# W1's transposes moved into another stage, K's stores on other queues, a third row buffer for W2 in a fused training step (long convolution gated with a squared-ReLU MLP)

## The chip, the cores and the metric

The kernel runs on one core of one Trainium2 chip. The metric is the device time of one execution in microseconds (us). TensorE is PE, its weight loads are PEld, VectorE is DVE, ScalarE is ACT, GpSimd is POOL and SyncE is SP. SP does no arithmetic here: it issues DMAs, as POOL and ACT also do beside their own work. Each engine takes its instructions in the order of its own queue, so an instruction that waits holds up all that stand behind it.

## The reference, cut to what matters

The input is a sequence of L = 2048 rows with D = 448 channels. A gate mixes the output of a long convolution (a state space model with 256 states per channel, whose kernel K is summed from powers and applied by FFT) with that of a dense block of hidden width F = 1792. Forward and all gradients are computed.

```python
g = sigmoid((u * gate_w).sum(-1, keepdims=True))
dt = exp(log_dt); P = exp((dt * A)[:, :, None] * arange(L))
K = einsum("dn,dnl,dn->dl", C, P, dt * B).real
a = irfft(rfft(pad(u)) * rfft(pad(K)))[:L] + u * Dskip
r = relu(x @ w1 + b1)
b = (r * r) @ w2 + b2
out = g * a + (1 - g) * b
_out, _vjp = jax.vjp(f, u, A_re, A_im, B_re, B_im, C_re, C_im, log_dt, Dskip, w1, b1, w2, b2, gate_w)
return out, *_vjp(grad_out)
```

Inputs and outputs are bf16.

## The kernel before

**Two jobs in one order.** The convolution and the dense block do not depend on each other until the end, so their work is interleaved by hand. The dense block is a Python generator `dense()` of small steps: `first_layer` (hidden rows r, written to DRAM as `rT_d`), `second_layer` (gradients of the hidden rows, written as `dhT_d`, and of the weights), `project(0, w2n)` (the output of the block) and `project(1, w1T)` (its gradient with respect to x). Each step has an entry in the list `cost`. `D_(want)` runs steps until their summed cost reaches a wanted share; the last `TAILN` = 6 steps are kept back and run by `N_(TAILN)` late in the tail. One projected tile is two steps of 7 matmuls each.

**The loop over chunks.** The 448 channels are worked off in 14 chunks c of 32. A period is a list of tokens, `PERIOD`, one for each chunk:

```python
PERIOD = """YS SA Z0 D R Y0 Y1 D Z1 Y2 D R Y3 Z2 D NX Y4 D Z3 KM KO
            LY WD P0 D P1 D X0 FY0 S FY1 FY2 X1 D R X2 D""".split()
```

YS and Y0 to Y4 build the table Y for chunk c on DVE (L1059, L1018 to L1021); there is one tile Y. KM makes K's terms from it with 128 matmuls (L1082), KO evicts them on ACT (L1089). LY issues four transposing DMAs of Y on SP (L1106) into the tile R; the next chunk's YS waits until they have landed. Z0 to Z3 multiply the transposed tables of the chunk before (matmuls L1144, eviction on ACT L1150); P0 and P1 are their products on DVE (L1159, L1161), S sums them (L1176, L1181). X and FY build the next tables. D stands for the dense steps.

**Queues and held loads.** The loads that the dense steps need are issued by `defer(key, f)`: it puts them into a list that `release()` empties at the tokens R and LY, so that the loads come out on SP's queue behind LY's transposes or ahead of them. Row loads for `project` are `load_rows2` (L881), with keys of 98 and more. `project` squares the loaded rows on ACT (L893) for its first half, evicts a tile on ACT (L908) and multiplies with w2 (natural) or with w1T, the transposed W1. Before, w1T is made by seven transposing DMAs on SP (`load_w1t`, L925), one each 256 columns of W1, spread over the tiles 0 to 5 of the first projection; the first is issued at the end of `second_layer`. The second layer turns W2 by transposes on PE from row buffers that POOL loads (`load_w2`, `turn_w2`); there are two such buffers. The squares of the first rows (L858) are done at the end of `second_layer`.

**The stores of K.** `k_store` writes K to DRAM (`k_d`, L1098) in two parts: after chunk 9 on POOL, and after the last chunk on POOL and SP, two each. `reload_k` reads it back in another layout (L1368, L1374, on both queues), `again` copies rows on DVE that are needed twice (L1440), one addition puts Dskip in (L1509), and `fwd1` transforms the result (L236, stores to gd). The last chunk's `T` token turns Y on PE instead of by DMA, and its Z (`back_z` with banks, L1148) is evicted by ACT and DVE in turn.

**The tail.** After fwd1 stand the `TAILN` dense steps, the loads of gd (`load_s1`, L250), the last P0 and P1, the parameter gradients `param_grads` (called in steps by `Pg`, L1459 to L1493) and `fwd2` (matmuls L260, evictions L211 and L222), whose results are multiplied (L1547, L1548) and transformed back.

Of the kernel before, what the change touches and what calls it, by code (L numbers as in the profile page):

```python
# [19 lines left out]
P = 128  # L20
# [3 lines left out]
DT = 4  # L24
# [295 lines left out]
def kernel(ctx, tc, A_u, A_A_re, A_A_im, A_B_re, A_B_im, A_C_re, A_C_im, A_log_dt, A_Dskip,  # L320
# [22 lines left out]
    dhT_d = dscr("dhT_d", F * L)  # L343

# [276 lines left out]
    w2b = [SB[:, 10240:10688], SB[:, 8208:8656]]  # L621
    w2T = [SB[:, 9216 + 512 * i:9728 + 512 * i].rearrange("p (a f) -> p a f", a=DT) for i in range(2)]
# [16 lines left out]
    def release():  # L639
        while held:  # L640
            held.pop(0)[1]()
# [79 lines left out]
    def first_layer():  # L721
# [6 lines left out]
        for j in range(FT):  # L728
# [29 lines left out]
    def load_w2(j):  # L758
        G_.dma_start(w2b[j % 2], bass.AP(tensor=B_w2.tensor, offset=B_w2.offset + j * P * D, ap=[[D, P], [1, D]]))

    def turn_w2(j):
        ps = K.ps(BK["t"], [P, DT, P], bf16)
        for dt in range(DT):
            for h in range(1 if dt < 3 else 2):
                T_.transpose(ps[64 * h:64 * h + DSZ[dt], dt], w2b[j % 2][:, dt * P:dt * P + DSZ[dt]], ident[:], tile_position=(0, 64 * h))
        S.copy(w2T[j % 2], ps[:])
        if j + 2 < FT:
            load_w2(j + 2)
# [51 lines left out]
    def second_layer():  # L820
# [44 lines left out]
        defer(99, lambda: load_w1t(0))  # L865
# [18 lines left out]

    def project(w, ws):
# [3 lines left out]
        def square(n, x):  # L889
            if w == 0:  # L890
                for b in slot_of(n):
                    v = b[:, :, P * x:P * x + P]
                    S.activation(v, v, ACT.Square)  # L893
        for x in range(2 * w):
            square(0, x)
        for n in range(8):
            for x in range(2):
# [11 lines left out]
                if n < 7:  # L909
                    square(n + 1, x)  # L910
# [4 lines left out]
                if x == 1:  # L915
# [4 lines left out]
                    if i < HP - 1:  # L920
                        defer(100 + i, lambda m=i + 1: load_w1t(m))
                yield

    def load_w1t(jp):
        nc.sync.dma_start_transpose(out=w1T[:, 2 * jp:2 * jp + 2], in_=B_w1[:, 256 * jp:256 * jp + 256])  # L925
# [13 lines left out]
    TAILN = 6  # L939
# [153 lines left out]
    def k_store(c):  # L1093

        if c in (9, NCH - 1):
            c0, n = (0, 5) if c == 9 else (5, 2)
            for g in range(NG):
                (G_ if c == 9 or g % 2 == 0 else nc.sync).dma_start(bass.AP(tensor=k_d, offset=112 * g + 16 * c0, ap=[[48 * D, NA], [D, NY], [1, 16 * n]]),  # L1098
# [34 lines left out]
    def back_z(c, yt, j, banks=None):  # L1133
# [12 lines left out]
        if banks:  # L1146
            for t in range(2):
                (S.copy if t == 0 else V.tensor_copy)(run(zbs[c, h][:, 0:1], 16 * (j % 2) + 1024 * t, [64, NA], [32, 2], [1, 16]), run(psz[t][:, 0:1], 0, [1, NA], [NA, 2], [32, 16]))  # L1148
# [143 lines left out]
    PERIOD = """YS SA Z0 D R Y0 Y1 D Z1 Y2 D R Y3 Z2 D NX Y4 D Z3 KM KO LY WD P0 D P1 D X0 FY0 S FY1 FY2 X1 D R X2 D""".split()  # L1292
    nd = PERIOD.count("D")

    def token(o, c):
# [13 lines left out]
        elif o == "R":  # L1309
            release()  # L1310
        elif o[0] == "L" and new:
# [41 lines left out]
    period(1, "YS Y0 Y1 Y2 Y3 Y4 D D D SP D WP KM KO D Z0 D Z1 D P0 Z2 D".split(), -nd)  # L1353
# [55 lines left out]
    G_.dma_start(Pt[:, 4096:7168], cdr["M2"].ap()[:, 0:3072])  # L1409
    Yf = Y[:].rearrange("p w t b -> p (w t b)")  # L1410
    slots = [KW[:, 7168:10752], KW[:, 10752:14336], R2[:, 7168:10752], R2[:, 12288:15872], hv[:, 0:3584], hv[:, 3584:7168], P2[:, 0:3584], Yf[:, 0:3584], Yf[:, 3584:7168]]
# [11 lines left out]
    period(NCH - 1, [o for o in PERIOD[:i] if o != "SA"])  # L1423
    D_(goal)
    release()
    assert done == total - TAILN
# [5 lines left out]
    for j in range(4):  # L1432
        back_z(NCH - 1, YTs[NCH - 1][j], j, NT[2 * (j % 2):2 * (j % 2) + 2])
    K.pairs = 3

    def again(p0, cp, j, m, i, step=1, rep_=1):
# [3 lines left out]
        cp(run(dst[:, 0, 0:1], 0, [step * D, rep_], [D, m], [1, D]), run(src[:, 0, 0:1], 0, [0, rep_], [D if step == 1 else 0, m], [1, D]))  # L1440
    Gt = Pt[:, 0:7168].rearrange("p (t d) -> p t d", d=D)
    tmps = [DBx[:, 7168:8192], hv[:, 7168:8192], Yf[:, 7168:8192], SB[:, 5120:6144], R2[:, 10752:11776], R2[:, 11776:12288]]
# [56 lines left out]
    again(64, V.tensor_copy, 2, 1, 0)  # L1499
    again(64, V.tensor_copy, 4, 1, 0, 4, 3)  # L1500
    again(64, V.tensor_copy, 5, 2, 1, 4, 3)
    again(64, V.tensor_copy, 7, 1, 3, 4, 3)
    for j, m, i in ((8, 4, 0), (4, 2, 0), (6, 1, 1), (12, 2, 2), (14, 1, 1), (15, 1, 7)):
        again(32, V.tensor_copy, j, m, i)
    got = {32: [0, 1, 2, 3, 0, 1, 1, 7, 0, 1, 2, 3, 2, 3, 1, 7], 64: [0, 1, 0, 3, 0, 1, 1, 3] + [0, 1, 1, 3] * 2}
    for p0, w in ((32, {0: 0, 8: 1, 4: 2, 12: 3, 16: 7}), (64, {0: 0, 8: 1, 16: 3})):
        assert [w[int(vp[p0, j]) - LT * p0] for j in JO] == got[p0]
    xv = xs.rearrange("p l (g c e) -> p l c g e", g=NG, e=16)
    V.tensor_tensor(out=xv[0:1, 0], in0=xv[0:1, 0], in1=dsk_bc[0:1].rearrange("o (c g e) -> o c g e", g=NG, e=16), op=ALU.add)  # L1509
# [186 lines left out]
```

## Time and profile before

| | us |
|---|---|
| median of 3 runs | 752.05 |
| fastest and slowest of them | 748.56, 754.67 |
| the profiled execution | 752.95 |
| its span | 751.1 |
| mean granted TensorE clock | 0.904 of full speed |

The span runs from the first to the last instruction of the profiled execution; the rest of its time lies around it. Times in the profile's views are counted from the span's start. Roughly, the loop over chunks runs from 214 to 603, with the second layer in the periods up to c = 7 and the two projections after them; the tail runs from 603 to the end. In the views, a group is given by line, engine, operation, and `out<-in` with the names of the tiles; several tiles share one buffer, so that w1T and the row buffers appear as S, U, P and F, and the transposed Y as R. A name such as `R<-Y` after an arrow is the instruction that ended a wait.

Some groups of the page for orientation (busy time in us and the mean of one in ns, then the idle time of the engine just before them):

```profile
L1018 DVE TENSOR_TENSOR Y<-Y,F 128x1024 bf16<-128x1024 bf16 (+3 forms) x70 | 48.0, 686 | 2.7
L905 PE MATMUL psN<-S,U 128*128 128x448 bf16 x140 | 29.0, 358 | 1.8 <-DMA S<-in_B_w_dram 1.8
L1059 DVE COPY Y<-rec 128x256 bf16<-128x256 bf16 x14 | 10.6, 755 | 21.5 <-DMA R<-Y 15.5
```

### The profile page before, as it was taken

The numbers are of one execution on the slowest core, as the hardware profiler recorded it, in microseconds if no ns is written. First come the engines' busy times: TensorE is split into PE (matmuls) and PEld (weight loads), VectorE is DVE, ScalarE is ACT, GpSimd is POOL, SyncE is SP. The second block draws the span as 40 slices with busy tenths as digits, with TensorE's granted clock in tenths as the row PEclk, the third lists the DMA queues.
The fourth block names the chain that finished last, engine by engine and source line by source line (L and its number), as shares of the span: only waits on it lengthen the run. The fifth ranks groups of instructions, "written<-read, shape, count | busy, mean of one in ns | idle before, by whom it ended". The sixth has DMA issues, their size and how long they took to land.

```text
span 751.1 us, 20458 instructions
## 1 busy us (share of the span) xinstructions
PE 621.1 (83%) x8556; PEld 337.4 (45%) x8597; DVE 564.7 (75%) x932; ACT 512.1 (68%) x873; POOL 171.6 (23%) x296
## 2 busy tenths in 40 slices
PE   5947968779999787999989997888969978687666
PEld 2412323323346453665665664555545664433111
DVE  1495586675698456899898997988699877959473
ACT  2895958587887576778777777777634535597555
POOL 2251112111263220211201201110100332411543
PEclk9887967879999899999999999999989988799758
DMA  9997586827773997997997989999999966998995
GB/s 211 220 280 243 195 294 240 291 103 285 283 263 134 249 256 214 200 249 203 219 209 216 240 137 240 244 198 245 218 186 234 276 165 199 389 333 297 333 327 147
DMA packets 197115, 177.77 MB, mean 237 GB/s; under 512 B 121534, under 2 KB 174039, under 8 KB 196895
## 3 DMA queue, kind: packets, MB, share of 16 engines
q1 hardware_dynamic: 173823, 113.11, 61.9%
q0 software_dynamic: 15632, 44.48, 19.3%
q10 hardware_dynamic: 7568, 18.88, 6.7%
q8 instruction: 67, 1.10, 0.6%
q14 instruction: 25, 0.20, 0.1%
HBM read 83.95 MB, written 64.32 MB: 197 GB/s over the span
## 4 chain that ended last, share of the span: by engine, by line
PE 28%; DMA 12%; DVE 10%; ACT 7%; issue 7%; POOL 1%; SPq 0%; POOLq 0%; ACTq 0%; DVEq 0%
PE psN L905 5%; PE psS L1176 5%; DMA R<-Y 3%; PE psN L661 3%; PE psX L1082 3%; PE psN L697 3%; DVE Y L1021 2%; DVE Y L1018 2%; DVE F L1019 2%; DMA U<-in_A_u_dram 2%; DMA S<-in_B_w_dram 2%; DMA hd<-F 2%; PE psN L296 1%; PE psF L1144 1%; ACT P L1150 1%
## 5 line engine op out<-in xcount | busy, mean ns | idle before, releaser
L697 PEld LDWEIGHTS <-U 128*128 128x128 bf16 x448 | 40.6, 99 | 42.4 <-issue 12.1
L1150 ACT CAST P<-psF 128x1024 bf16<-128x1024 f32 x52 | 53.1, 1021 | 7.0 <-PE psF L1144 6.8
L1018 DVE TENSOR_TENSOR Y<-Y,F 128x1024 bf16<-128x1024 bf16 (+3 forms) x70 | 48.0, 686 | 2.7
L661 PEld LDWEIGHTS <-S 128*128 128x128 bf16 x336 | 30.2, 101 | 44.1 <-issue 18.5
L1021 DVE TENSOR_TENSOR Y<-Y,F 128x1024 bf16<-128x1024 bf16 (+3 forms) x70 | 48.1, 687 | 2.4
L697 PE MATMUL psN<-S,U 128*128 128x449 bf16 x224 | 47.8, 355 | 0.2 <-issue 0.2
L661 PE MATMUL psN<-S 128*128 128x512 bf16 x153 | 46.3, 415 | 1.9 <-issue 1.0
L1019 DVE TENSOR_TENSOR F<-Y,F 128x1024 bf16<-128x1024 bf16 (+3 forms) x70 | 47.2, 674 | 0.0
L697 PE MATMUL psX<-D,U 128*128 128x448 bf16 x160 | 37.3, 370 | 2.0 <-ACT D L703 2.0
L689 ACT ACTIVATE U<-psN 128x1024 bf16<-128x1024 bf16 x35 | 36.1, 1032 | 1.5 <-PE psN L688 1.5
L1183 POOL DMA_DIRECT2D s_d<-st x28 | 14.0, 506 | 97.6 <-ACT st L1181 97.6
L905 PEld LDWEIGHTS <-U 128*128 128x128 bf16 x252 | 24.2, 100 | 24.7 <-issue 4.7
L676 ACT ACTIVATE U<-psN,b_f 128x512 bf16<-128x512 f32 x48 | 31.0, 688 | 6.0 <-PE psN L664 4.3
L1144 PEld LDWEIGHTS <-R 41*128 41x128 bf16 x1792 | 27.0, 93 | 17.8 <-issue 15.0
L1144 PE MATMUL psF<-S,R 41*128 41x32 bf16 x1664 | 29.4, 174 | 5.9 <-ACT P L1150 5.9
L661 PE MATMUL psN<-K,S 128*128 128x512 bf16 x100 | 27.6, 391 | 5.6 <-issue 3.2
L905 PE MATMUL psN<-S,U 128*128 128x448 bf16 x140 | 29.0, 358 | 1.8 <-DMA S<-in_B_w_dram 1.8
L296 PEld LDWEIGHTS <-cb_MI 64*128 64x128 bf16 x256 | 15.6, 98 | 32.1 <-issue 23.6
L1176 PE MATMUL psS<-ident,P 128*64 128x128 bf16 x896 | 27.4, 219 | 0.0
L1176 PEld LDWEIGHTS <-M 128*64 128x64 bf16 x896 | 25.7, 110 | 3.0 <-issue 1.5
L1059 DVE COPY Y<-rec 128x256 bf16<-128x256 bf16 x14 | 10.6, 755 | 21.5 <-DMA R<-Y 15.5
L1176 PEld LDWEIGHTS <-P 128*64 128x64 bf16 x896 | 25.9, 110 | 0.0
(417 smaller groups left out, 1688.7 us busy)
## 6 DMA issues: line engine op xcount, KB each, us to landing
sp<-K ACTq DMA_DIRECT2D x8, 896.0 KB, 4.2
rT_d<-U POOLq DMA_DIRECT2D x11, 512.0 KB, 3.0
hd<-F SPq DMA_DIRECT2D x11, 448.0 KB, 14.1
U<-rT_d SPq DMA_DIRECT2D x9, 512.0 KB, 4.7
X<-gd SPq DMA_DIRECT2D x5, 896.0 KB
U<-dhT_d SPq DMA_DIRECT2D x5, 896.0 KB, 9.6
rec_d<-F ACTq DMA_DIRECT2D x2, 1920.0 KB
hd<-st ACTq DMA_DIRECT2D x8, 448.0 KB, 4.8
```

The costliest lines, as they stand in the source:

```text
L296: nc.tensor.matmul(ps[kk2][:, 0:D], lhsT=m[r0:r0 + 64], rhs=x[r0:r0 + 64, 2 * q2 + ii, ri, :], start=(k == 0), stop=(k == len(terms) - 1), ...
L661: T_.matmul(pss[k][:], lhsT=w[:, dt], rhs=x(2 * half + k)[:, dt], start=(dt == 0), stop=False, skip_group_check=True)
L676: S.activation(r[:, 512 * lb:512 * lb + 512], pss[k][:], ACT.Relu, bias=b1_f[:, j:j + 1])
L689: S.activation(hn[j % 2][:, 8 * th:8 * th + 8, :], ps[:], f)
L697: T_.matmul(ps[:, 0:w], lhsT=hn[j % 2][:, t, :], rhs=rhs[:, t, :], start=(t == 0), stop=(t == LT - 1))
L905: T_.matmul(ps[:, 0:D], lhsT=src[j][:, P * x:P * x + P], rhs=ws[:, j, :], start=(j == 0), stop=(j == FT - 1))
L1018: V.tensor_tensor(out=run(yb, dst, [64, X2], [d0[1], n // d0[1]], [1, d0[1]]), in0=run(yb, 0, [64, X2], *src), in1=pr, op=ALU.mult)
L1019: V.tensor_tensor(out=run(vb, 0, [n, X2], [d0[1], n // d0[1]], [1, d0[1]]), in0=run(yb, 0, [64, X2], *src), in1=pi, op=ALU.mult)
L1021: return V.tensor_tensor(out=hi, in0=hi, in1=run(vb, n, [2 * n, W2], [-n, 2], [1, n]), op=ALU.add)
L1144: T_.matmul(psz[t][:, 32 * b:32 * b + 32], lhsT=yt[64 * t:64 * t + NY, b, :], rhs=DKc[64 * t:64 * t + NY, c % 2, 16 * (j % 2) + b].rearran ...
L1150: S.copy(run(zbs[c, h][:, 0:1], 16 * (j % 2), [1024, 2], [64, NA], [32, 2], [1, 16]), run(psF[:, 0, 0:1], 0, [512, 2], [1, NA], [NA, 2], [ ...
L1176: T_.matmul(sps[64 * h:64 * h + 64, cc, r, :], lhsT=Q[h][r][:, 1024 * t + 64 * a:1024 * t + 64 * a + 64], rhs=(nident if r == 0 and t == 1 ...
```

## The change

1. **W1.** Tokens r and rw are new. They release only held loads with a key below 98; the first and the second R of a period become rw and r, and the third stays. At R in the periods c = 2 to 5, and at rw in c = 3 to 5, `turn_w1` transposes 256 columns of W1 by DMA on SP into a staging tile of two buffers, and POOL stores it to a new DRAM tensor `w1T_d`. Two plain loads on SP (`load_w1t`, 7 blocks of 448 columns per partition each) fetch it during the first projection, after its second and fourth row.
2. **W2.** Three row buffers; the third load is issued earlier, and the load of row j + 3 follows the turning of row j.
3. **Squares.** `square(0, 0)` is at the end of the second layer, `square(0, 1)` at the start of the projection. Before, both stood at the end of the second layer.
4. **K's last stores** go to the queues of ACT and SP instead of POOL and SP. KM and KO of the last chunk are put ahead of the last dense step before the tail; the reload is issued right after the last T; the copies `again` and the addition of Dskip stand ahead of `back_z`, whose evictions are all on ACT.
5. **The tail.** `TAILN` is 8 instead of 6. P0 and P1 of the last chunk and `Pg(8)` stand ahead of these steps; two of the spectra loads (`load_sx`), `load_st(1)` and a load of the table M2 change their place in the queues, and some buffers move.
6. In the period of c = 1 one D is put ahead of KM instead of behind Z1.

```diff
+    w1T_d = dscr("w1T_d", F * D)
...
-    def release():
-        while held:
+    def release(below=1000):
+        while held and held[0][0] < below:
             held.pop(0)[1]()
...
                 if j == FT - 1:
+                    load_w2(2)
                     defer(j, load_u)
...
-        if j + 2 < FT:
-            load_w2(j + 2)
+        if j + 3 < FT:
+            load_w2(j + 3)
...
-        for x in range(2):
-            v = slot_of(0)[0][:, :, P * x:P * x + P]
-            S.activation(v, v, ACT.Square)
+        square(0, 0)
...
-        defer(99, lambda: load_w1t(0))
...
-        for x in range(2 * w):
-            square(0, x)
+        if w == 0:
+            square(0, 1)
...
-                    if i < HP - 1:
-                        defer(100 + i, lambda m=i + 1: load_w1t(m))
+                    if i in (1, 3):
+                        defer(100 + i, lambda m=i // 2: load_w1t(m))
...
-    def load_w1t(jp):
-        nc.sync.dma_start_transpose(out=w1T[:, 2 * jp:2 * jp + 2], in_=B_w1[:, 256 * jp:256 * jp + 256])
+    def turn_w1(jp):
+        st = K.t("st", [P, 2, D], bufs=2)
+        nc.sync.dma_start_transpose(out=st[:], in_=B_w1[:, 256 * jp:256 * jp + 256])
+        G_.dma_start(bass.AP(tensor=w1T_d, offset=256 * jp * D, ap=[[D, P], [P * D, 2], [1, D]]), st[:])
+
+    def load_w1t(h):
+        nc.sync.dma_start(w1T[:, HP * h:HP * h + HP], bass.AP(tensor=w1T_d, offset=HP * h * P * D, ap=[[D, P], [P * D, HP], [1, D]]))
...
-    TAILN = 6
+    TAILN = 8
...
-                (G_ if c == 9 or g % 2 == 0 else nc.sync).dma_start(...)
+                (G_ if c == 9 else nc.scalar if g % 2 == 0 else nc.sync).dma_start(...)
...
-                (S.copy if t == 0 else V.tensor_copy)(run(zbs[c, h][:, 0:1], ...
+                S.copy(run(zbs[c, h][:, 0:1], ...
...
-    PERIOD = """YS SA Z0 D R Y0 Y1 D Z1 Y2 D R Y3 Z2 D ...
+    PERIOD = """YS SA Z0 D rw Y0 Y1 D Z1 Y2 D r Y3 Z2 D ...
...
         elif o == "R":
             release()
+            if new and 2 <= c < 6:
+                turn_w1(c - 2)
+        elif o[0] == "r":
+            release(98)
+            if o == "rw" and new and 3 <= c < 6:
+                turn_w1(c + 1)
...
-    period(NCH - 1, [o for o in PERIOD[:i] if o != "SA"])
+    last = [o for o in PERIOD[:i] if o != "SA"]
+    m = len(last) - last[::-1].index("D") - 1
+    period(NCH - 1, last[:m] + last[m + 1:] + ["KM", "KO"])
     D_(goal)
-    release()
+    period(NCH - 1, "P0 P1 WD T".split())
+    reload_k()
+    release()
     sx[0, 0] = load_sx(0, 0, 5)
-    period(NCH - 1, "KM KO P0 P1".split())
-    reload_k()
-    period(NCH - 1, "WD T S".split())
+    period(NCH - 1, "S".split())
...
     K.fwd1(lambda j: xv[:, JO.index(j)], gd[2], stage=stg)
+    for o in ("P0", "P1"):
+        token(o, NCH)
+    Pg(8)
     N_(TAILN)
```

More of the change, by code (lines that the diff above doesn't have):

```diff
@@ L620 @@
     dws = SB[:, 7184:8208].rearrange("p (a f) -> p a f", a=DT)
-    w2b = [SB[:, 10240:10688], SB[:, 8208:8656]]
-    w2T = [SB[:, 9216 + 512 * i:9728 + 512 * i].rearrange("p (a f) -> p a f", a=DT) for i in range(2)]
+    w2b = [SB[:, 10240:10688], SB[:, 9232:9680], SB[:, 9680:10128]]
+    w2T = [SB[:, 8208 + 512 * i:8720 + 512 * i].rearrange("p (a f) -> p a f", a=DT) for i in range(2)]
     w1T = SB[:, 0:FT * D].rearrange("p (j d) -> p j d", d=D)
@@ L883, with square @@
     nbk = 0
+    def square(n, x):
+        for b in slot_of(n):
+            v = b[:, :, P * x:P * x + P]
+            S.activation(v, v, ACT.Square)
     def project(w, ws):
         nonlocal nbk
[L889 to L893, printed above, removed]
-        for x in range(2 * w):
-            square(0, x)
+        if w == 0:
+            square(0, 1)
         for n in range(8):
@@ L908, in project @@
                 S.copy(br[w][:, t], ps[:, 0:D])
-                if n < 7:
+                if w == 0 and n < 7:
                     square(n + 1, x)
@@ L1352, in period @@
                 token(o, c)
-    period(1, "YS Y0 Y1 Y2 Y3 Y4 D D D SP D WP KM KO D Z0 D Z1 D P0 Z2 D".split(), -nd)
+    period(1, "YS Y0 Y1 Y2 Y3 Y4 D D D SP D WP D KM KO D Z0 D Z1 P0 Z2 D".split(), -nd)
     for lb in range(4):
```

57 lines of the change are left out of this document (27 added, 30 removed).

## The prediction

> **What bounds the kernel now.** I read the page first. No engine fills the span: TensorE (PE) leads, yet VectorE (DVE) paces the middle.
>
> ```profile
> span 751.1 us, 20458 instructions
> PE 621.1 (83%) x8556; PEld 337.4 (45%) x8597; DVE 564.7 (75%) x932; ACT 512.1 (68%) x873; POOL 171.6 (23%) x296
> ```
>
> The sum below is made against this execution: 752.95 us, 1.85 more than its span and 0.9 above the median of the runs, 752.05 (748.56 to 754.67). About 1% is what a measurement of this kernel can tell from no change.
>
> Second, the busy time by stretches, cut at the first instruction of each chunk's tile Y (L1059). Columns: stretch, length, busy time and instructions of PE, weight loads, DVE, ACT, POOL, then granted clock, DMA share, GB/s. The rows are the periods of c = 3 to 11.
>
> ```profile
> core 0: us, PE busy (x) PEld busy (x) DVE busy (x) ACT busy (x) POOL busy (x), PEclk, DMA share, GB/s
> 317.20:344.10 26.90, 25.81 (x483) 16.48 (x487) 25.13 (x36) 20.28 (x37) 3.71 (x7) 1.00 1.02 252
> 344.10:372.30 28.20, 26.55 (x538) 17.43 (x542) 24.73 (x36) 22.93 (x41) 5.49 (x10) 1.00 1.00 203
> 372.30:399.40 27.10, 24.59 (x474) 15.83 (x479) 24.70 (x35) 18.98 (x36) 3.49 (x6) 0.94 0.96 218
> ...
> 425.10:450.80 25.70, 23.65 (x495) 15.79 (x496) 24.75 (x37) 20.11 (x38) 2.97 (x6) 1.00 0.87 193
> 450.80:480.50 29.70, 25.68 (x504) 16.17 (x503) 23.27 (x34) 21.30 (x31) 5.94 (x11) 0.94 1.00 232
> 480.50:509.20 28.70, 24.46 (x485) 15.32 (x476) 24.06 (x36) 22.30 (x28) 3.83 (x6) 1.00 1.20 226
> 509.20:540.25 31.05, 28.61 (x517) 17.46 (x514) 23.39 (x33) 24.25 (x32) 3.13 (x6) 0.95 1.20 219
> ```
>
> The row 425.10:450.80 shows the floor: DVE works 24.75 of 25.70. The three rows after it, where the projection runs and W1 is turned, take 4.0, 3.0 and 5.35 longer though DVE has less to do (23.27 to 24.06). Those 12.35 us are what the middle can give.
>
> Third, who DVE and PE wait for between 250 and 660 us (total, times, longest):
>
> ```profile
> DVE Y L1059 <- DMA R<-Y: 15.5, 5, 7.0
> DVE M L1159 <- ACT P L1150: 13.7, 4, 5.6
> DVE F L789 <- DMA U<-rT_d: 4.1, 1, 4.1
> ```
> ```profile
> PE psN L236 <- DVE F L1509: 5.4, 1, 5.4
> PE psN L260 <- DMA R<-gd: 4.2, 1, 4.2
> PE psN L765 <- DMA S<-in_B_w_dram: 2.9, 1, 2.9
> ```
>
> The first row is the loop's tie: the next chunk's Y may be written once the four transposes of the last Y (LY, into R, L1106) have landed. Fourth, the timeline of SP's queue around two of those (start, duration, engine, line, operation), and the group of W1's transposes with their min/median/max in ns:
>
> ```profile
> L925 SPq DMA_TRANSPOSE S<-in_B_w_dram x7: 2246/3687/6200, 478.9 to 537.0; - x7
> ```
> ```profile
> 482.06 0.52 SPq L881 DMA_DIRECT2D U<-rT_d  x1
> 482.63 6.20 SPq L925 DMA_TRANSPOSE S<-in_B_w_dram  x1
> ...
> 517.32 4.45 SPq L925 DMA_TRANSPOSE S<-in_B_w_dram  x1
> 521.87 13.73 SPq L1106 DMA_TRANSPOSE R<-Y  x4
> 355.59 12.90 SPq L1106 DMA_TRANSPOSE R<-Y  x4
> ```
>
> A transpose holds SP while it runs; the queue is in order. LY of c = 10 starts only when the W1 transpose ends at 521.77, and takes 13.73.
>
> **W1.** Removed from the project periods: seven transposes, about 7 x 3.69 = 26 us of SP's queue by the median. In their place stand seven in the periods of c = 2 to 5, seven stores on POOL to DRAM and two plain loads.
>
> Period 480.50: W1's 6.20 us pushes LY past the end of Y. The ideal is 25.7, so 3.0 can go; I take 2.5. Period 509.20: the late LY and its 13.73 end in the longest DVE wait, 7.0. Up to 5.35 can go; the loads of the projection's rows stay on the queues (DMA share 1.20), so I take 4. The late candidate after that is DVE itself. Together -6.5, between -8.35 and 0.
>
> The two plain loads are 7 x 448 columns each. The nearest row is the plain row load above, 0.52 on SP, so 1 us in total. This I cost at nothing, between 0 and 2 x 3.69 = 7.4 if they held the queue like transposes; their cover is SP's free time after LY.
>
> [...]
>
> In the second layer a period of c = 3 to 5 lasts (26.90 + 28.20 + 27.10)/3 = 27.4 and LY takes 12.90, so SP has 14.5 us outside LY. Two transposes take 7.4 there (12.4 at the longest), and the order puts them behind the release of held loads (token R, and in c = 3 to 5 also the new rw after Z0), before Y4 is done. Plain DMAs take some 0.5 each. It fits, but not with room for a long one. I cost each of four periods at 0.75, +3. Bounds: 0, and 3.65 each (31.05 - 27.4, as if each became what c = 10 was), +14.6.
>
> The stores wait on POOL for a transpose to land. Queued behind them are the next chunk's record loads, W2's loads and the gradient stores. A store's own price comes from the stage stores:
>
> ```profile
> L1183 POOL DMA_DIRECT2D s_d<-st x28 | 14.0, 506 | 97.6 <-ACT st L1181 97.6
> ```
>
> Seven times 0.51 is 3.5 us of an engine that is busy 3.5 to 5.5 us in these periods, so the price is zero; at the far end each of the seven holds a load by one transpose's 3.69 and DVE waits it out, a part of the 14.6 already.
>
> **Releases.** r and rw release nothing with a key of 98 or more, so the project's row loads leave at R or behind LY. Before, every release freed them in their turn, as the row load at 482.06 shows between two transposes. Tiles of rows 5, 7, 12 and 13 may come later. The nearest row is the wait for a first tile below, 3.81; four times that is +15 if DVE waited each out, but the loop waits on Y, and PE and ACT can catch up beside DVE's 25.7. I take +1.5.
>
> **The squares** at the first project period. DVE's longest wait for ACT stands at 470.30, in the period of 29.70:
>
> ```profile
> 467.24 0.53 ACT L908 CAST K<-psN 128x448 bf16<-128x448 f32 x1 [3.81 <-PE psN L905]
> 467.66 1.70 ACT L893 ACTIVATE U<-U 128x1792 bf16<-128x1792 bf16 x1
> 469.26 1.00 ACT L1150 CAST P<-psF 128x1024 bf16<-128x1024 f32 x1
> ```
> ```profile
> 470.30 1.23 DVE L1159 TENSOR_TENSOR M<-P,R 128x2048 bf16<-128x2048 bf16 x1 [5.57 <-ACT P L1150]
> ```
>
> ACT's eviction of Z, for which DVE waits, stands behind the first projected tile and a square. The change does square(0,0) alone, square(0,1) after it, and the tokens shift by one tile, so that Z's and K's evictions come ahead of that tile. The 5.57 goes; what is late next is the loop, at 25.7, 4.0 us shorter than this period. I take -3 (0 to -4.0).
>
> **W2.** A third row buffer and an earlier load remove PE's 2.9 for L765. DVE's F L789 waits 4.1 for another load there, which the change leaves. So 0, -2.9 at most. The token list of period 1, with one more dense step ahead of KM, I put at 0 (+-2).
>
> Middle: -6.5 + 3 + 1.5 - 3 = -5, with the hopeful end at -12 (all project periods at 25.7) and the far one in the rivals.
>
> **The tail.** Rows: K's stores, the reload that waits for them (idle before it in brackets), what DVE does.
>
> ```profile
> L1098 POOL DMA_DIRECT2D k_d<-X x6: 677/708/734, 504.6 to 604.9; - x6
> L1098 SPq DMA_DIRECT2D k_d<-X x2: 621/653/685, 603.9 to 604.7; - x2
> ```
> ```profile
> 610.65 1.24 POOL L1368 DMA_DIRECT2D F<-k_d  x2 [5.01 <-DMA k_d<-X]
> ```
> ```profile
> 613.09 2.65 DVE L1148 CAST P<-psN 128x512 bf16<-128x512 f32 x4 [3.70 <-PE psN L1144]
> 615.69 0.06 DVE L1445 MEMSET dlog<- 128x4 f32 x1
> 615.76 4.12 DVE L1440 COPY F<-F 64x448 bf16<-64x448 bf16 x10
> ```
>
> The stores move from POOL and SP to ACT and SP. Issue falls by 2 x (0.708 - 0.653) = 0.1, and ACT starts right after its own eviction; the 5.01 of landing stays. [...] I take 0.1.
>
> DVE's four Z evictions (2.65) go to ACT and the copies stand ahead of them, so they may start as the reload lands. But the projected tile that now stands behind KM (2.65, from the evictions at 635.29 and 637.94 below) delays the transposes and sums on PE, and ACT then has eight evictions to do before it can empty fwd1's first tile. So fwd1's start, and with it the 5.4 wait of L236, gains 1 (0 to 2.65).
>
> ```profile
> 635.29 0.53 ACT L908 CAST D<-psN 128x448 bf16<-128x448 f32 x1 [2.12 <-PE psN L905]
> 637.94 0.53 ACT L908 CAST D<-psN 128x448 bf16<-128x448 f32 x1 [2.12 <-PE psN L905]
> 638.37 0.72 ACT L1463 ACTIVATE D<-R,dtc 128x512 f32<-128x512 bf16 x1
> ```
> ```profile
> 639.12 0.69 DVE L1459 TENSOR_TENSOR Y<-D,R 128x512 f32<-128x512 f32 x1 [3.72 <-ACT D L1463]
> ...
> 646.15 0.62 DVE L211 CAST R<-psN 128x448 bf16<-128x448 f32 x1
> ```
>
> After fwd1 DVE waits 3.72 for an ACT step that is queued behind the projected tiles; then the parameter gradients (Pg) keep it to 646.15, and fwd2's first eviction on DVE comes after them. The change puts Pg(8) ahead of those tiles, so the 3.72 goes, and fwd2's eviction is next bound by L260, whose input lands 4.2 us into a PE hole. The one tile more after fwd1 costs 2.65 inside that hole: nothing, or up to 2.65 without it. I take -3 (0 to -3.72). Moving M2's load on POOL and the sx loads on SP I cost at nothing, at worst one row load, 0.52 each.
>
> Tail: -0.1 - 1 - 3 = -4.1, between +2.65 and -6.4 (0 - 2.65 - 3.72; with a landing gone, -11).
>
> Sum: 752.95 - 5 - 4.1 = 743.9, say 744.
>
> **The rivals.** First, *given back* (0.23): a W1 transpose costs in c = 2 to 5 what it frees in c = 9 and 10, whether because the DMA engines bound both stages or because both have the same room. Against it, the 14.5 us outside LY; for it, a DMA share of 0.96 to 1.02 there, and that those periods already stand 1.7 above 25.7. Then +3 becomes +6.5, and with late rows +1.5 and squares -3 the middle is -1.5: 752.95 - 1.5 - 4.1 = 747.4, within 1%. [...]
>
> Second, *the tail keeps its length* (0.1): fwd1 waits for reload and ACT, and fwd2 for the gd loads. Then 752.95 - 5 = 748.
>
> Third, *SP's queue blocks the second layer* (0.13), slower than before: transposes are still running when Y4 ends, in four periods, and the row loads come late behind LY. It decides once the W1 transposes and plain loads of a period exceed the 14.5 us outside LY, that is if both transposes take over 6 each, as one here did. Price: +14.6, row waits 2 x 3.81 = +7.6, and the gains -9.5 and -4.1 remain: 752.95 + 8.6 = 761.6.
>
> Fourth, *all project periods at the floor* (0.12): -12 and -6.4, with +3: 737.6.
>
> Fifth, *the change doesn't do what it says* (0.02): squares and tokens stay behind the first tile, and 5.57 stays, 747.
>
> **How the numbers follow.** The forecast (0.40) is 744, by itself 738 to 750. Faster by over 1% is under 744.5: a little over half of the forecast, 0.24; nearly all of the fourth, 0.12; of the first and second, whose tail term reaches down to -6.4 and beyond, 0.12: 0.48. Slower than 759.6: of the third 0.10, of the others 0.03: 0.13. The rest is 0.39. The range from 733 to 759 reaches over the first, second, fourth and fifth cases and leaves out some 0.14 above and 0.05 below.
>
> **What would show it.** Right: no W1 transpose between 470 and 540; LY of c = 9 and 10 starting within 0.2 of Y4's end; project periods of 26 to 27; no ACT wait over 2 at the first of them; Pg ahead of the last tiles. Wrong: periods of c = 2 to 5 longer than 28; LY there behind a W1 transpose; PE or ACT waiting over 3 for row loads; fwd1 starting no sooner after KM than the 19.1 us from 601.30 to 620.40:
>
> ```profile
> 601.30 2.05 PE L1082 MATMUL psX<-Y,R 128*32 128x41 bf16 x128 [1.12 <-DVE Y L1021]
> ...
> 620.40 1.65 PE L236 MATMUL psN<-F,cb_F1BD 128*128 128x448 bf16 x4 [5.42 <-DVE F L1509]
> ```

## The result and the profile after

The changed kernel takes 776.15 us (median of 6 runs, 770.38 to 782.42) against 753.88 for the kernel before (6 runs): a ratio of 1.0277, 95% interval 1.0219 to 1.0335. The ratio leaves out the changed kernel's run of 782.42, which was a disturbed one. The forecast was 744, and its range ended at 759: slower, where faster was forecast, and beyond the third rival's 761.6 as well.

The profiled execution's span is 774.1 against 751.1, 23.0 more. Below is the page's table of engines for the changed kernel, then its busy time by stretches, cut like the rows of before (columns: stretch, length, busy time and instructions of PE, weight loads, DVE, ACT, POOL, then granted clock, DMA share, GB/s). The line of Y's first instruction is L1063 now.

```profile
PE 634.9 (82%) x8556; PEld 342.2 (44%) x8597; DVE 563.3 (73%) x928; ACT 512.6 (66%) x877; POOL 175.5 (23%) x301
```
```profile
321.90:350.80 28.90, 26.23 (x511) 16.82 (x516) 24.68 (x35) 21.22 (x38) 4.93 (x8) 0.94 1.02 228
350.80:383.80 33.00, 25.21 (x483) 17.54 (x482) 25.24 (x37) 17.16 (x30) 4.93 (x8) 0.90 1.15 231
383.80:415.90 32.10, 28.55 (x512) 17.83 (x515) 24.99 (x35) 23.38 (x43) 7.49 (x13) 0.95 1.01 214
...
468.50:493.70 25.20, 21.02 (x467) 14.34 (x464) 22.89 (x33) 14.12 (x24) 3.15 (x5) 1.00 0.86 192
493.70:529.70 36.00, 28.53 (x506) 16.94 (x507) 24.13 (x35) 27.98 (x37) 4.29 (x8) 0.86 0.89 199
529.70:554.90 25.20, 22.89 (x425) 14.12 (x422) 23.82 (x35) 17.83 (x23) 4.27 (x8) 0.93 1.01 206
554.90:587.70 32.80, 26.93 (x501) 16.40 (x501) 23.51 (x33) 17.09 (x27) 2.42 (x4) 0.95 1.18 266
```

The work is the same (DVE 563.3 against 564.7); what grew is waiting. The rows are c = 3, 4, 5 and c = 8 to 11. Placed beside before, the 23.0 divides so (lengths in us; the first instruction of c = 1 stands 1.4 later already):

| stretch | before | after | difference | forecast |
|---|---|---|---|---|
| c = 1 and 2 | 79.1 | 82.3 | +3.2 | 0 for c = 1, +0.75 for c = 2 |
| c = 3 to 5 | 82.2 | 94.0 | +11.8 | +2.25 |
| c = 6 and 7 | 51.4 | 52.6 | +1.2 | 0 |
| c = 8 | 29.7 | 25.2 | -4.5 | -3 |
| c = 9 | 28.7 | 36.0 | +7.3 | -2.5 |
| c = 10 | 31.05 | 25.2 | -5.85 | -4 |
| c = 11 | 24.8 | 32.8 | +8.0 | +1.5 in all for late rows |
| c = 12 | 25.3 | 24.3 | -1.0 | 0 |
| c = 13 to the end | 160.8 | 162.1 | +1.3 | -4.1 |

The gains that were forecast in c = 8 and c = 10 came. They are buried under four losses. The waits of DVE in the changed kernel between 200 and 690 us (total, times, longest) name them:

```profile
DVE M L1163 <- ACT P L1154: 21.8, 6, 13.3
DVE Y L1063 <- DMA R<-Y: 19.3, 9, 4.7
DVE K L913 <- ACT K L907: 13.1, 2, 9.0
```

Of the first row's wait 13.3 is one wait in c = 1, taken up under e1. The third row is as good as new: in the kernel before, the same wait came to 0.87 in all. L913 adds the bias to a projected tile; it is queued on DVE ahead of Y's build. Followed back from the wait of 9.0 in c = 9 it leads to SP's queue. Timeline of SP, ACT and DVE there, the changed kernel (start, duration, engine, line, operation, idle before and what ended it):

```profile
479.70 12.19 SPq L1110 DMA_TRANSPOSE R<-Y  x4
491.94 0.57 SPq L880 DMA_DIRECT2D U<-rT_d  x1
```
```profile
497.67 1.70 ACT L887 ACTIVATE U<-U 128x1792 bf16<-128x1792 bf16 x1 [12.18 <-DMA U<-rT_d]
```
```profile
503.41 0.62 DVE L913 TENSOR_TENSOR K<-K,b_bc 128x896 bf16<-128x896 bf16 x1 [9.00 <-ACT K L907]
```

And SP in the kernel before, the same load of the projection's second row:

```profile
456.25 0.37 SPq L881 DMA_DIRECT2D U<-rT_d  x1
461.96 11.88 SPq L1106 DMA_TRANSPOSE R<-Y  x4
```

Before, the load stood ahead of the LY of c = 8; now it stands behind it, and ACT, PE and DVE wait in turn. This load is not a held one and has nothing to do with the release rule. What moved it is `TAILN`: it sets the goal over which all dense steps are spread, so 8 instead of 6 puts each step a little later against the tokens, and the last step of the second layer, which issues this load, fell just behind LY.

In the second layer the four transposes of LY take longer, 19.44 and 16.58 us in c = 4 and 5 against 12.90 and 11.76. First who waited for W1's transposes (L925 of the changed kernel: in all, times), then POOL, ACT and SP in c = 4 and 5:

```profile
  POOL w1T_d L926: 16.0, 3
```

```profile
360.84 0.72 POOL L926 DMA_DIRECT2D w1T_d<-st  x1 [23.93 <-DVE Y L1025]
361.55 0.56 POOL L1032 DMA_DIRECT2D F<-rec_d  x1
```
```profile
367.32 0.36 ACT L1040 ACTIVATE F<-F 128x192 bf16<-128x192 bf16 x1 [5.51 <-DMA F<-rec_d]
```
```profile
362.54 19.44 SPq L1110 DMA_TRANSPOSE R<-Y  x4
397.09 16.58 SPq L1110 DMA_TRANSPOSE R<-Y  x4
```

POOL has issued nothing for 23.93 us when the store of W1 leaves at 360.84; the record load queued behind it leaves at 361.55, just ahead of LY, and ACT waits 5.51 for that. (In the kernel before, POOL's gaps in these periods reach 14.4.)

### The profile page after: what moved, and what is told of

It reads as the page before. It is cut to its first block, busy times and chain, and to the rows that moved or that the text cites. A ratio compares the mean times of both kernels' runs of the same rounds, so it can differ in the third digit from the quotient of the medians.

```text
span 774.1 us, 20479 instructions
## 1 busy us (share of the span) xinstructions
PE 634.9 (82%) x8556; PEld 342.2 (44%) x8597; DVE 563.3 (73%) x928; ACT 512.6 (66%) x877; POOL 175.5 (23%) x301
## 4 chain that ended last, share of the span: by engine, by line
PE 29%; DMA 13%; DVE 9%; ACT 8%; issue 7%; POOL 1%; SPq 0%; POOLq 0%; ACTq 0%; DVEq 0%
PE psS L1180 5%; PE psN L904 4%; PE psN L698 4%; DMA R<-Y 4%; PE psN L662 3%; PE psX L1086 3%; DVE Y L1025 2%; DVE Y L1022 2%; DVE F L1023 2%; DMA gd<-X 2%; DMA out_dram<-S 2%; PE psN L689 1%; PE psF L1148 1%; DMA st<-in_B_w_dram 1%; ACT U L690 1%
## 5 line engine op out<-in xcount | busy, mean ns | idle before, releaser
L698 PEld LDWEIGHTS <-U 128*128 128x128 bf16 x448 | 41.6, 101 | 43.8 <-issue 14.7
L662 PEld LDWEIGHTS <-S 128*128 128x128 bf16 x336 | 29.9, 100 | 52.3 <-issue 26.4
L698 PE MATMUL psN<-S,U 128*128 128x449 bf16 x224 | 49.9, 366 | 0.0
L904 PEld LDWEIGHTS <-U 128*128 128x128 bf16 x252 | 25.6, 106 | 34.9 <-ACT U L887 8.8
L904 PE MATMUL psN<-D,U 128*128 128x448 bf16 x112 | 26.8, 399 | 8.0 <-ACT U L887 8.0
L904 PE MATMUL psN<-S,U 128*128 128x448 bf16 x140 | 32.2, 388 | 0.0
L1163 DVE TENSOR_TENSOR M<-P,X 128x2048 bf16<-128x2048 bf16 x14 | 17.1, 1221 | 16.7 <-ACT P L1154 16.7
L1180 PEld LDWEIGHTS <-M 128*64 128x64 bf16 x896 | 27.2, 114 | 3.1 <-issue 2.4
```

The lines of the kernel that those rows point to most:

```text
L662: T_.matmul(pss[k][:], lhsT=w[:, dt], rhs=x(2 * half + k)[:, dt], start=(dt == 0), stop=False, skip_group_check=True)
L698: T_.matmul(ps[:, 0:w], lhsT=hn[j % 2][:, t, :], rhs=rhs[:, t, :], start=(t == 0), stop=(t == LT - 1))
L904: T_.matmul(ps[:, 0:D], lhsT=src[j][:, P * x:P * x + P], rhs=ws[:, j, :], start=(j == 0), stop=(j == FT - 1))
L1180: T_.matmul(sps[64 * h:64 * h + 64, cc, r, :], lhsT=Q[h][r][:, 1024 * t + 64 * a:1024 * t + 64 * a + 64], rhs=(nident if r == 0 and t == 1 ...
```

## The experiments

Each was run beside the kernel before on one chip; the ratio is to it. The changed kernel itself was timed beside the kernel before only for the result, so what a repair is worth is a difference of two ratios, each known to some 0.6%. Lengths of periods are read from one profiled execution of each kernel, which by itself wanders. The start of c = 1, where all kernels but the early-W1 ones do the same, lies between 236 and 242. The stretch of c = 3 to 5 takes 94.0, 91.0, 95.9 and 86.3 in the changed kernel, e1, e2 and e13, whose programs are the same there.

**e1: the period of c = 1 as before.**
```diff
-"... D D D SP D WP D KM KO D Z0 D Z1 P0 Z2 D"
+"... D D D SP D WP KM KO D Z0 D Z1 D P0 Z2 D"
```


> The changed kernel with the token list of the period of c = 1 as it was before (the dense step behind Z1 again, not ahead of KM). In the trace of the changed kernel KM of c = 1 starts at 259.7 instead of 249.1, because the dense step now ahead of it on PE waits 8.7 for ACT, which waits 10.6 for a load of dk_d; the period's first instruction to that of c = 3 takes 82.4 instead of 79.1. Theory A, the token order is the cause: KM of c = 1 starts near 250 again, the stretch is 78 to 80, and the time is 3 to 4 us below the changed kernel's 776, near 773. Theory B, the stretch is long for another reason (W2's third buffer and its earlier loads): KM stays near 259 or the stretch stays at 82, and the time is 775 to 777.

1.0171 (1.0111 to 1.0231), 769.2. c = 1 and 2 take 77.7 instead of 82.3, and KM of c = 1 starts at 251.0 instead of 259.7. Theory A holds. The ratio is 1.1% lower, more than these 4.6 us account for, but the two intervals touch. The chain is in the changed kernel's rows: ACT's copy of S waits for a load and stands ahead of the dense step's eviction, PE's dense step waits for that eviction, and KM is queued behind the dense step.

```profile
253.99 1.05 ACT L1129 COPY S<-K 128x512 bf16<-128x512 bf16 x1 [10.59 <-DMA K<-dk_d]
```
```profile
255.68 1.86 PE L662 MATMUL psN<-S 128*128 128x512 bf16 x4 [8.74 <-ACT F L677]
```

**e2: every row released at rw and r.**
```diff
         elif o[0] == "r":
-            release(98)
+            release()
```


> The changed kernel with r and rw releasing every held load, rows of the projection too; all else stays, W1 in the second layer included. Theory A, the rule below 98 is the cause: the row loads leave SP ahead of LY again, DVE's waits of 9.0 and 4.1 for K's eviction in the projection go, the periods of c = 9 and c = 11 fall from 36.0 and 32.8 to 26 to 28, and the time is 12 to 15 us below 776, at 761 to 764. Theory B, the row loads are late because the DMA engines are full there: the two periods stay above 31 and the time above 770. Theory C, rows ahead of LY push LY instead: the waits of DVE for R<-Y grow by as much, the two periods fall but their neighbours rise, and the time is 768 to 774.

1.0146 (1.0087 to 1.0206), 766.7. c = 11 falls from 32.8 to 25.7, c = 9 only to 34.5. So without the rule below 98 the loss in c = 11 is gone, and that in c = 9 is not; the expectation was half right.

**e3: W1 turned in the projection as before. e4: W1's stores on SP behind the next LY.**
```diff
-        G_.dma_start(bass.AP(tensor=w1T_d, ...), st[:])
+        w1s.append((jp, st))
...
             YTs[c] = [load_yt(j) for j in range(4)]
+            store_w1()
             release()
```


> The changed kernel with W1 turned as before: seven transposing DMAs on SP in the first projection, nothing of W1 in the second layer, no DRAM copy; r and rw still release only keys below 98. Theory A, W1's part costs the second layer what was measured: the stretch from the first instruction of c = 3 to that of c = 6 falls from 94.0 to 82 to 85; the project periods of c = 9 to 11 lose 3 to 8 by the transposes; the time is 3 to 8 below 776, at 768 to 773. Theory B, the second layer is long for another reason (r and rw, W2's buffers): the stretch stays above 90 and the time rises by the project's part, to 779 or more.

> The changed kernel with W1's seven transposes where the change has them, but their stores to DRAM not on POOL right behind them: they are issued on SP behind the next LY, when the transposes have long landed. In the changed kernel POOL stands up to 8 us in each of these stores, and the record loads, W2 loads and output stores behind them come out in a bunch beside LY, whose four transposes take 19.4 and 16.6 in c = 4 and 5. Theory A, the store that waits on POOL is the cost: the stretch from c = 3 to c = 6 falls from 94.0 to 83 to 87, LY takes under 14.5, and the time is 7 to 11 below 776, at 765 to 769. Theory B, the transposes themselves are (SP's queue and the DMA engines' time): the stretch stays at 91 to 95, LY over 16 in two periods, and the time at 773 to 777.

e3: 1.0127 (1.0048 to 1.0206); c = 3 to 5 takes 83.4 instead of 94.0, as theory A of e3 has it. But c = 10 lost 3.1 (28.3), c = 9 kept its 34.9: again not W1's doing. e4: 1.0174 (1.0123 to 1.0225); c = 3 to 5 takes 89.1, and the LY of c = 4 still 17.46. That is neither theory. The time is 1% lower, but the stretch does not show where: 89.1 lies between the 86.3 and the 95.9 of kernels that have the stores on POOL. LY is long with no store ahead of it on POOL. What the stores cost is left open.

**e5: TAILN 6. e6: the tail's part alone on the kernel before, with TAILN 8.**
```diff
-    TAILN = 8
+    TAILN = 6
```


> The changed kernel with TAILN 6 instead of 8, nothing else. TAILN also sets the goal over which the dense steps are spread, so 8 puts every step of the loop a little later against the tokens; with 6, on SP, the load of the second row of the projection stands ahead of the LY of c = 8 again, as do the row loads at the LY of c = 10, and K's and P's loads of the second layer stand ahead of the LY of c = 4. Theory A, this shift is behind the long periods of c = 9 and c = 11 (36.0 and 32.8), which releasing all rows cured in the second alone: they fall below 30 both, that of c = 4 (33.0) by 2 or more, the 5.57 wait for ACT in the period of c = 8 may come back (25.2 becomes 28 to 30), and the time is 9 to 15 below 776, at 761 to 767. Theory B, the rule below 98 alone is behind it: c = 9 stays above 33 and the time at 772 to 777.

> The kernel before with the change's tail alone: TAILN 8, K's stores on ACT and SP, the new order around the last chunk, Z's evictions on ACT, P0, P1 and Pg(8) ahead of the last dense steps; W1, W2, squares, the token lists and the release rule as before. Theory A, TAILN's shift does harm in the loop by itself: some of the periods of c = 4, 9 and 11 grow by 3 to 7, the time is 5 to 12 above the kernel before, at 759 to 766. Theory B, the shift harms only with r, rw and W1's transposes: the periods stay within 2 of before, and with the tail from the first instruction of c = 13 at 160 to 162 against 160.8 the time is 751 to 757.

e5: 1.0133 (1.007 to 1.0196), 762.1: one number is worth half of the loss. c = 9 falls to 26.5 and c = 11 to 27.2, c = 8 rises to 28.1. So in c = 11 it takes both: the rule below 98 with TAILN 6 costs little (27.2 here), and TAILN 8 without the rule costs little (25.7 in e2, 26.1 in e6). e6: 1.0053 (1.0023 to 1.0083), 757.9: on the kernel before, without W1's move and without the release rule, c = 9 rises from 28.7 to 35.7 and c = 8 falls from 29.7 to 25.4. Theory A in both, though e6's loss of 0.5% is less than the 5 us that it foresaw at least.

**e7 and e8: four things mended together (TAILN 6 and 8).** TAILN, the period of c = 1, the release, the stores of W1.

> The changed kernel with four things undone or moved: TAILN 6, the period of c = 1 as before, every row released by r and rw, W1's stores on SP behind LY. What is left of the change: W1 turned in the second layer, W2's third buffer, the square, the tail's order. Theory A, the four account for the loss and each works by itself: the time is 745 to 756, at or below the kernel before. Theory B, W1's transposes in the second layer cost by themselves: the stretch from c = 3 to c = 6 stays above 87 and the time is 757 to 764.

> The same with TAILN 8, as the change has it. Theory A of the shift: 5 to 9 above the run with TAILN 6, through the periods of c = 4 and c = 9. Theory B, the shift is harmless once the rows are released: within 3 of it.

e7: 0.9988 (0.9953 to 1.0022); e8: 1.0147 (1.0084 to 1.021). With all four the whole loss is gone, with TAILN 8 left in half of it is there. In e7 c = 3 to 5 still takes 89.3 against 82.2 before: W1's part costs there with its stores on SP as well.

**e9: W1's part alone. e10: the tail's order alone, TAILN 6.** On the kernel before.

> The kernel before with the change's first part alone: W1 turned in the periods of c = 2 to 5 and stored by POOL, loaded plainly in the projection, the squares split; every row released at rw and r, TAILN 6, tail, W2 and the period of c = 1 as before. Theory A, W1's move gives the project periods less than it costs the second layer: c = 3 to 6 takes 88 to 94 against 82.2, c = 9 to 12 takes 78 to 82 against 84.6, and the time is 2 to 8 above before, at 756 to 762. Theory B, what was lost came from TAILN and the release rule alone and W1 gains: below 752.

> The kernel before with the tail's new order alone and TAILN left at 6: K's stores on ACT and SP, KM ahead of the last dense step, the copies ahead of Z, Z on ACT, P0, P1 and Pg(8) ahead of the dense steps. The loop stays as before. Theory A, the tail's order gains what the prediction said: from the first instruction of c = 13 to the end 155 to 157 against 160.8, and the time 747 to 751. Theory B, it gains only with the fourth tile in the tail: 159 to 161 and 753 to 756.

e9: 0.9982 (0.9948 to 1.0017): c = 3 to 5 90.8 (+8.6), c = 8 to 11 109.0 against 114.3 (-5.3). Most of the cost is given back, as the first rival had it. Of theory A the stretches hold, but not the loss: by the ratio it is neither gain nor loss. e10: 0.9949 (0.9914 to 0.9985): c = 13 to the end takes 157.8, between the two theories, and the time is 0.5% lower, 3.9 us of before's 756.42 in that comparison.

**e11 and e12: W1 turned ahead of the loop (TAILN 6 and 8).** On e10, with W2's and the squares' part.
```diff
+    w1st = [SB[:, 10240 + 896 * i:11136 + 896 * i]... for i in range(2)]
...
     load_y(0)
+    for jp in range(HP):
+        turn_w1(jp)
+        if jp > 0:
+            store_w1(jp - 1)
+    store_w1(HP - 1)
```


> The run before with W1 as well, but turned on SP ahead of the loop (after the first record loads, in a buffer of S that lies idle there), stored on SP, and loaded plainly in the projection; W2's third buffer and the split squares as in the change; R as before, TAILN 6. Theory A, W1's transposes are only harmful next to LY: the periods c = 2 to 6 are as before within 2, c = 9 to 12 takes 78 to 82 against 84.6, and the time is 742 to 748, below both kernels. Theory B, the DMA engines are the bound and the transposes cost their time anywhere: the first instruction of c = 1 comes 3 or more later than 236 to 241, and the time is 748 to 755.

> The same with TAILN 8. Theory A, the shift puts the load of the projection's second row behind the LY of c = 8 here too, where neither W1 nor the release rule can be the cause: the period of c = 9 takes 33 or more, that of c = 8 25 to 26, and the time is 3 to 9 above the run with TAILN 6. Theory B, the shift is harmless without the other parts: within 3 of it.

e11: 0.9908 (0.9873 to 0.9942), 751.2 against 756.4: the lowest ratio of all, below the kernel before and the changed one, though above theory A's 742 to 748. Its interval overlaps that of e10 (0.9914 to 0.9985), so what W1 adds to the tail's order by being turned early is not shown by the time. c = 3 to 5 takes 80.0, c = 10 26.4 against 31.05. Its stretch of c = 10, and its group of W1's transposes (min/median/max in ns):

```profile
514.20:540.60 26.40, 25.57 (x506) 16.13 (x505) 23.46 (x34) 23.07 (x30) 3.16 (x6) 1.00 1.09 222
```
```profile
L926 SPq DMA_TRANSPOSE S<-in_B_w_dram x7: 1215/1240/2519, 147.1 to 178.6; - x7
```

The same transposes hold SP 1.24 here where they held it 3.69. Theory A for the loop; but c = 1 starts at 244.2, 2 to 8 later than in the kernels without early W1: theory B's later start is there. That the DMA engines are the bound is not shown. e12: 1.0056 (1.0026 to 1.0085): c = 9 takes 35.3 with neither W1 nor the rule beside it. Theory A.

**e13 and e14: one load back ahead of LY.** On the changed kernel, and on e12.
```diff
         elif o == "LY" and new:
+            if c == 8:
+                N_(1)
             YTs[c] = [load_yt(j) for j in range(4)]
```


> The changed kernel with one dense step run ahead of the LY of c = 8 instead of right after it. On SP this moves a single instruction: the load of the projection's second row stands ahead of those four transposes and no longer behind them. Theory A, that load behind LY is what makes the period of c = 9 take 35 to 36: it falls to 26 to 30, ACT's wait of 10 to 12 for U<-rT_d goes, and the time is 5 to 8 below the changed kernel, near 769. Theory B, TAILN does its harm all over the loop: c = 9 stays above 33, or its gain appears as loss in c = 8 and 10, and the time is 773 or more.

> The kernel with W1 turned ahead of the loop and TAILN 8, and the same one step ahead of the LY of c = 8. Theory A, c = 9 falls from 35.3 to 26 to 30 with c = 8 still under 28, and the ratio to before goes from 1.0056 to 0.990 to 0.997. Theory B, the step costs in c = 8 what it saves in c = 9: ratio above 1.000.

e13: 1.0115 (1.0064 to 1.0165), 764.6. SP's queue and the stretch of c = 9:

```profile
471.30 0.37 SPq L880 DMA_DIRECT2D U<-rT_d  x1
474.97 12.90 SPq L1110 DMA_TRANSPOSE R<-Y  x4
```
```profile
490.90:517.10 26.20, 21.27 (x417) 13.29 (x415) 23.84 (x35) 18.49 (x25) 1.17 (x3) 0.87 1.02 214
```

36.0 has become 26.2, and one DMA has changed its place on SP. c = 8 keeps a little more than half of its gain (27.1) and c = 11 its loss (33.0). This settles c = 9 of the changed kernel. e14: 0.9978 (0.9937 to 1.0019), just outside theory A, which fails for c = 9. ACT's wait for U<-rT_d is gone there too, but c = 9 takes 33.9 all the same, by another way:

```profile
494.06 3.71 SPq L932 DMA_DIRECT2D S<-w1T_d  x1
498.07 17.32 SPq L1113 DMA_TRANSPOSE R<-Y  x4
```
```profile
520.35 0.74 DVE L1066 COPY Y<-rec 128x256 bf16<-128x256 bf16 x1 [9.09 <-PE psN L904]
```

All row loads and one of W1's leave right ahead of LY, and LY takes 17.32 where e13, with the rule below 98, has 11.38. DVE's 9.09 is put down to a PE instruction that came last, but DVE starts 4.96 after LY's last issue, so it may well have waited for LY. The release rule of the change thus seems to help c = 9 (26.2 in e13 and 26.5 in e5 with it, 30.4 in e7 without), and with TAILN 8 it harms c = 11.

**e15: three repairs on the changed kernel** (the step of e13, e2's release, e1's order).

> The changed kernel with three small repairs: the one step ahead of the LY of c = 8, every row released at rw and r, the period of c = 1 as before. W1 in the second layer with its stores on POOL, TAILN 8 and the tail as the change has them. Theory A, the three carry most of the loss and W1's part the rest in c = 3 to 6 (88 to 96 against 82.2): ratio 1.000 to 1.010. Theory B, W1's part is the larger: ratio above 1.012.

1.004 (1.0001 to 1.0078). Theory A: what is left of 2.8% is 0.4%. Taken singly the same three repairs come to 1.6, 1.3 and 1.1%, more than the 2.4% that they are worth together, so their prices do not add. The profiled execution took 764.31, the median of the kernel is 757.15, and no period is read from it.

## Why the prediction was wrong, point by point

**The step that failed.** "the tokens shift by one tile, so that Z's and K's evictions come ahead of that tile." The shift was taken as a gain in c = 8 and looked at nowhere else. The gain was right: -3 forecast, -4.5 measured, and it goes when TAILN goes back (28.1 in e5). But the shift acts on the whole loop, DMA issues included, and one load fell behind LY: +7.3 in c = 9 instead of -2.5. Moving that one load back is worth 1.6% (after, e13). Four pairs of kernels that differ in TAILN alone put the price of the whole shift at 1.0277 - 1.0133 = 1.4% (after, e5), 1.6% (e8, e7), 1.5% (e12, e11) and 1.0% (e6, e10): 8 to 12 us. The prediction compared the queue's order only where the diff touched it.

**Releases, "+1.5".** Measured +8.0 in c = 11. The reason given, that "PE and ACT can catch up beside DVE's 25.7", was the fault: L913 stands in DVE's own queue ahead of Y's build, so a late row is a late Y:

```profile
562.16 0.62 DVE L913 TENSOR_TENSOR K<-K,b_bc 128x896 bf16<-128x896 bf16 x1 [4.09 <-ACT K L907]
```

In that period DVE waits another 4.46 for LY, which starts only when Y is done. The bound of 3.81 for each tile was also too short; a load behind LY waits out LY's 11.0 to 13.8 (c = 8 to 12). e2 and e5 show that in c = 11 the rule and TAILN 8 do harm only together, and e14 hints that the rule is worth having in c = 9.

**W1 in the second layer, "+3".** This term was sized too small. Measured +11.8, within the bound of +14.6; but that is one execution. Over the runs the split is clean: with W1 there, c = 3 to 5 takes 86.3 to 95.9, 90.5 in the mean (after, e1, e2, e4, e5, e7, e8, e9, e13); without, 80.0 to 84.4, 81.7 in the mean (before, e3, e6, e10, e11, e12, e14). So some 9 in these three periods. Room on SP's queue was counted, 14.5 us, and that was there: no LY starts late behind a W1 transpose (in c = 3 to 6 of the changed kernel LY starts 0.06 to 0.42 after Y's last instruction ends). So the third rival, which foresaw a loss there, had the wrong way to it. It is LY itself that gets longer: in c = 4 it takes 14.0 to 23.2 with W1 there (19.44 in the changed kernel, 17.46 in e4) and 12.2 to 16.0 without (12.90 before, 15.96 in e3). "The price is zero" for the stores on POOL is not settled by e4. How the cost divides between the transposes, the stores and the traffic that they push together was not separated.

**Project periods, "-6.5".** c = 10 gave -5.85 for -4. c = 9 would have given some without the load: e13 has 26.2, e5 26.5, against 28.7. W1's move by itself nets nothing (e9, 0.9982): the first rival described W1's part well. It had +6.5 and -6.5; e9 has +8.6 and -5.3. What one of W1's transposes held SP differs by place (medians): 3.69 in the projection before, at a DMA share of 1.20 (478 to 541); 1.80 in the second layer of the changed kernel, where the rows of c = 3 to 5 show 1.01 to 1.15; 1.24 in e11, from 147 to 179, a stretch with a share of 0.55 in the kernel before, which has none of them there. The plain row load at 482.06 took 0.52.

**The period of c = 1, "0 (+-2)".** Measured +3.2; e1 is 1% faster. The chain of three queues was not followed, though ACT's wait for K<-dk_d could be seen in the profile of before.

**The tail, "-4.1".** By itself it came near: e10 gives 0.5%, 3.9 us, and c = 13 to the end 157.8 instead of 160.8. That is luck in part, because its terms were off both ways. In the changed kernel's profiled execution the tail gave +1.3; in the fourteen kernels with the new tail (after, e1 to e8, e10 to e14) it takes 155.3 to 164.0, against 160.8 before and 160.0 in e9.

K's stores were undersized. Between the first of them and the first reload on SP pass 631.45 - 627.13 = 4.32 in the changed kernel, and 4.25 to 4.81 in all with the new tail; it was 610.27 - 603.95 = 6.32 before and 5.38 in e9. With ACT's queue in POOL's place this interval was 0.6 to 2.1 shorter, not 0.1. That the issue alone gets shorter and "the 5.01 of landing stays", on which the 0.1 rests, is shown by no run. A part of what took this gain back in the changed kernel stands right behind KM:

```profile
626.50:632.00 5.50, 5.31 (x18) 2.07 (x15) 1.56 (x2) 0.67 (x2) 0.04 (x1) 0.54 0.32 39
```
```profile
626.48 5.33 PE L904 MATMUL psN<-S,U 128*128 128x448 bf16 x14
...
643.88 2.00 PE L236 MATMUL psN<-F,cb_F1BD 128*128 128x448 bf16 x4
```

The tile moved behind KM takes 5.33 at a granted clock of 0.54, where 2.65 was forecast, and fwd1 starts 20.93 after KM (622.95) instead of 19.10. This is the longest of all: in the other thirteen the tile takes 3.4 to 4.9 and fwd1 starts 16.2 to 19.9 after KM, so the gain of 1 that was forecast here mostly comes. Pg moved as forecast, but fwd2 is then late by its loads:

```profile
659.55 0.68 DVE L1486 TENSOR_TENSOR Y<-D,R 128x512 f32<-128x512 f32 x1
...
670.38 0.63 DVE L211 CAST Y<-psN 128x448 bf16<-128x448 f32 x1 [3.72 <-PE psN L260]
```

SP's loads of gd, in the changed kernel and before:

```profile
664.40 0.81 SPq L250 DMA_DIRECT2D Y<-gd  x2
```
```profile
637.37 0.81 SPq L250 DMA_DIRECT2D R<-gd  x2
```

They leave 20.52 after fwd1's start, before 16.97, so from that start to DVE's eviction pass 26.50, before 25.75. From there to the end the changed kernel is only 1.2 shorter. All kernels with the new tail share this: the gd loads leave 18.3 to 24.7 after fwd1's start, against 17.0 and 17.6 (e9). The term behind it seems to be "Moving M2's load on POOL and the sx loads on SP I cost at nothing". Two sx loads of 896 KB each stood behind the gd loads and now leave ahead of fwd1's stores (R<-sp, Y<-sp before). A third, U<-sp, and M2's load of 768 KB left before KM and now leave just ahead of fwd1. The sx loads in the changed kernel, then before:

```profile
636.30 1.13 SPq L1423 DMA_DIRECT2D U<-sp  x1
641.63 2.50 SPq L1423 DMA_DIRECT2D R<-sp  x2
```
```profile
597.07 2.55 SPq L1414 DMA_DIRECT2D U<-sp  x1
639.46 0.92 SPq L1414 DMA_DIRECT2D Y<-sp  x2
```

About fwd1 the DMA share and the GB/s (the last two columns) rise, the changed kernel and then before:

```profile
644.00:655.00 11.00, 9.01 (x33) 3.58 (x33) 8.61 (x14) 8.81 (x17) 3.99 (x6) 0.84 1.02 390
```
```profile
621.00:631.00 10.00, 8.98 (x38) 3.89 (x37) 8.65 (x14) 7.87 (x14) 3.48 (x5) 0.88 0.61 197
```

The stores of gd, which the gd loads wait for, then take 7.8 us to land (median) instead of 5.3. The price of a load was counted on SP's queue alone, and not as traffic. That these loads are the cause is argued from the rows; no run moved them back.

**W2** removed PE's wait of 2.9 and showed nothing by itself; no run tried it alone.

## What to carry to other kernels

A constant that spreads filler work over a hand-written order moves every step of it, with its DMA issues: compare the whole queue of each engine that issues DMAs, and look for loads that change sides of a long blocking instruction. Work that "can catch up" has to be followed into the queue of the engine that paces the loop. Room on a queue did not tell where W1's transposes fit: the second layer had 14.5 us of it on SP, and c = 3 to 5 took 90.5 in the mean with them there. Of W1's three places, ahead of the loop was the one with which the loop kept its length (80.0 in e11), though a gain in time by itself is not shown. A load that is brought forward should be priced by its traffic, too, and not only by its issue: about fwd1 the DMA share was 1.02 instead of 0.61 here, and the stores of gd took 7.8 us to land instead of 5.3, though no run shows that the loads moved there are the cause.

## What the runs showed of the hardware

Transposing DMAs of one size held SP for different times: 224 KB of W1 took 1.24 us (median) ahead of the loop (e11), 1.80 in the second layer (after) and 3.69 in the projection (before), and LY's four took 11.0 to 19.4 in one execution (after). The granted clock fell to 0.54 (626.5 to 632) for the tile right after KM in the changed kernel. From 612 on PE had only these gaps ahead of it:

```profile
622.95 1.58 PE L1086 MATMUL psX<-Y,R 128*32 128x41 bf16 x97 [1.08 <-DVE Y L1025]
625.89 0.65 PE L1086 MATMUL psX<-Y,R 128*32 128x41 bf16 x31 [1.36 <-issue]
```

From 624 to 626.5 the granted clock was 0.66 already, from 621 to 624 still 1.00. In e6 a gap of 5.00 went before KM, and the tile behind it took 4.08, less than the 5.33 here. What sets the lower clock off was not tried.
